# Two unused 32-byte tiles in the SBUF of an attention and gated-MLP kernel

## The chip, the cores and the metric

The kernel runs on one core of one Trainium2 chip. A core has a matrix engine (PE, with its weight loads shown as PEld), a vector engine (DVE), a scalar engine (ACT), a GpSimd engine (POOL) and a queue engine (SP) that only issues transfers. The on-chip memory that the engines compute from is the SBUF, 128 partitions wide; matmuls write to the PSUM. The metric is the device time of one execution in microseconds. Three runs of the kernel before gave 789.4, 789.5 and 789.96 us; the median is 789.5 us.

## The reference

Shapes: 8 batches, 8 heads, 576 rows of 64 elements, 32 memory slots. The attention output of one batch is 576 x 512, and all of them make 4608 rows of the gated MLP with 1536 inner columns.

```python
a = softmax(phi, over the rows)                # [b, h, 576, 32]
k_m = einsum('bhsm,bhsd->bhmd', a, k)
v_m = einsum('bhsm,bhsd->bhmd', a, v)
attn = softmax(q @ k_m.T / 8, over the slots)
x = (attn @ v_m) with the heads side by side   # [4608, 512]
gate = 1 / (1 + exp(-(x @ w_gate)))
out = (gate * (x @ w_val)) @ w_out             # [4608, 512]
```

All inputs and outputs are float32; the weights `w_gate`, `w_val`, `w_out` reach the kernel as 64-bit words, which it turns into float32 on the chip (`to_f32`).

## The kernel before

**The work.** The inner dimension 1536 is cut into 12 blocks of 128 (`f` = 0 to 11, constant `NFT`), and a batch's 576 rows into two halves: 256 rows (`c` = 0) and 320 rows (`c` = 1, of which the last 64 are a leftover). For each batch the attention weights `at` (softmaxed scores, transposed) are made once. Instead of forming x, the kernel multiplies `v_m` into the weight block: `make_u` (line 426) streams `wg`, the converted gate and value weights, past weights from `vT`, and gives U. `gate_half` (line 463) then streams `at` past U: 12 matmuls of 256 or 320 columns. Its sigmoid and product give `g`. `out_half` (line 499) streams a block of `w_out` past `g`: 6 matmuls of 512 columns, which accumulate in the banks `acc`. `out_left` (line 545) does the same for the leftover rows of two batches at a time.

**Two words for a number.** U, `at`, `g` and `w_out` are each kept as a high and a low part (`hi`, `lo`); a product is hi x hi, hi x lo and lo x hi, so each logical product takes three matmuls. These tiles have the type fp32r.

**The order.** 96 steps (batch, block) are written out by hand at line 753: batches 0 to 3 go in turns of four blocks with partial sums kept in DRAM (`part`), batches 4 to 7 go through all 12 blocks at once. A step is a gate half, an output half that belongs to a half three places earlier (`LAG` = 3), a second gate half and another output half; on every second step `make_u` stands between. The order on the matmul queue is fixed by `in_turn` (line 127), that of transfers by `move` (line 113). `convert` jobs for the weights end at step 30; the side work of the next batches' attention is put between the halves by `sides` (line 725). `again` (line 418) loads the `at` tiles of a batch back a turn before they are used.

**The placing.** Three pools hold the SBUF tiles, opened in the order `keep`, `att`, `moe` (lines 66 to 69); a pool `conv0`, later `late` and `conv1`, comes behind. A pool's tiles lie one behind the other in the order in which they are first asked for, each rounded up to a multiple of 32 bytes in a partition. By the sizes, this is where the start of each tile lies, in bytes past a multiple of 64 and of 128:

| pool: tiles | start, bytes | past 64 | past 128 |
|---|---|---|---|
| keep: `ident`, `tails`, `wg` | 16512, 17024, 18048 | 0 | 0 |
| keep: `wo_hi`, `wo_lo` (blocks 0 to 7) | 67200, 83584 | 0 | 0 |
| keep: `kT`, `vT` (5 buffers), `at_hi`, `at_lo` (2 each) | 99968 to 124544 | 0 | 0 |
| att: `z`, then `ph`, `kvt`, `kvm`, `q` | 124544, then 124576 on | 0, then 32 | 0, then 32 |
| att: `e` | 156864 | 0 | 64 |
| moe: `u_hi`, `u_lo`, `sg`, `g_lo`, `g_hi`, `left`, `wo_raw`, `row` | 161824 on | 32 | 32 |
| late: `wo2_hi`, `wo2_lo` (blocks 8 to 11) | 208672, 216864 | 32 | 32 |

All slices that the matmuls of the main loop take start a multiple of 256 bytes behind the start of their tile. The two w_out tiles differ only in the block they serve:

```python
wos = {0: [keep.tile([P, NE, DM], F32R, name=f"wo_{part}") for part in ("hi", "lo")]}   # NE = 8
def wo_of(f):
    return [t[:, f % NE, :] for t in wos[f // NE]]
```

The second is made at line 207, when the last conversion buffers are free. Names in the profile leave out numbers, so `wo_hi` there stands for `wo_hi` and `wo2_hi`.

Of the kernel before, what the change touches and what calls it, by code (L numbers as in the profile page):

```python
# [9 lines left out]
F32 = mybir.dt.float32  # L10
# [7 lines left out]
P = 128  # L18
# [34 lines left out]
def attn_moe_kernel(  # L53
# [12 lines left out]
    keep = ctx.enter_context(tc.tile_pool(name="keep", bufs=1))  # L66
    dram = ctx.enter_context(tc.tile_pool(name="dram", bufs=1, space=bass.MemoryType.DRAM))
    sb = ctx.enter_context(tc.tile_pool(name="att", bufs=1))
# [18 lines left out]
    ident = keep.tile([P, P], F32, name="ident")  # L87
    make_identity(nc, ident)

    tails = keep.tile([P, NG, P], F32, name="tails")  # L90
    nc.vector.memset(tails, 0.0)


    wg = keep.tile([P, NFT, NKT, 256], F32, name="wg")
    wos = {0: [keep.tile([P, NE, DM], F32R, name=f"wo_{part}") for part in ("hi", "lo")]}

    def wo_of(f):
# [746 lines left out]
```

## Time and profile before

| | |
|---|---|
| median of three runs | 789.5 us |
| profiled execution, first to last instruction (span) | 788.0 us |
| PE busy | 750.2 us, 95% |
| PEld busy | 617.4 us, 78% |
| DVE busy | 436.4 us, 55% |
| ACT busy | 335.8 us, 43% |
| moved by DMA | 93.17 MB, 118 GB/s on average |
| mean granted clock of the matrix engine | 0.981 |

The page gives the profiled execution's span alone, not its time from outside; the span lies 1.5 us under the median of the runs. Busy time counts an instruction from its start to its end, and matmuls overlap, so that the time of one in the trace is longer than the distance to the next. The pace of matmuls is therefore read from the starts, or from the rows of the chain of waits, in which a stretch of matmuls of one kind is merged into one row with its length and count.

### The profile page before, as it was taken

The numbers are of one execution on the slowest core, as the hardware profiler recorded it, in microseconds if no ns is written. First come the engines' busy times: TensorE is split into PE (matmuls) and PEld (weight loads), VectorE is DVE, ScalarE is ACT, GpSimd is POOL, SyncE is SP. The second block draws the span as 40 slices with busy tenths as digits, with TensorE's granted clock in tenths as the row PEclk, the third lists the DMA queues.
The fourth block names the chain that finished last, engine by engine and source line by source line (L and its number), as shares of the span: only waits on it lengthen the run. The fifth ranks groups of instructions, "written<-read, shape, count | busy, mean of one in ns | idle before, by whom it ended". The sixth has DMA issues, their size and how long they took to land.

```text
span 788.0 us, 13851 instructions
## 1 busy us (share of the span) xinstructions
PE 750.2 (95%) x5658; PEld 617.4 (78%) x5658; DVE 436.4 (55%) x840; ACT 335.8 (43%) x789; POOL 15.8 (2%) x34
## 2 busy tenths in 40 slices
PE   6866999989999999999999999999999999999997
PEld 4654777678788888887888878878888888888886
DVE  2878656887677775455654653365234553343432
ACT  3445455545644434332633543346333443333322
POOL 0000000000100000000000000000000000000000
PEclk9897899999999999999999999999999999999999
DMA  9683555564755555333253133002000100010001
GB/s 343 240 294 129 188 191 201 205 226 167 240 213 195 188 177 182 122 108 114 67 198 148 54 104 121 1 29 86 1 1 2 54 14 1 1 55 1 1 1 67
DMA packets 31231, 93.17 MB, mean 118 GB/s; under 512 B 3520, under 2 KB 4544, under 8 KB 29120
## 3 DMA queue, kind: packets, MB, share of 16 engines
q1 hardware_dynamic: 22528, 69.22, 24.3%
q0 software_dynamic: 4032, 14.68, 5.6%
q10 hardware_dynamic: 4608, 8.39, 3.5%
q8 instruction: 44, 0.72, 0.4%
q14 instruction: 19, 0.16, 0.1%
HBM read 69.73 MB, written 22.54 MB: 117 GB/s over the span
## 4 chain that ended last, share of the span: by engine, by line
PE 77%; DVE 9%; ACT 6%; DMA 5%; issue 2%; SPq 0%; ACTq 0%; DVEq 0%; POOLq 0%
PE pu_t L133 47%; PE acc L133 30%; DMA words<-in_wgv_dram 3%; ACT L108 2%; ACT ph L108 1%; DVE u_lo L123 1%; DVE q L394 1%; DVE e L373 1%; DVE sg L489 1%; DVE e L358 1%; DVE at_lo L123 1%; DMA part<-row 1%; ACT sg L108 1%; ACT e L108 1%; DMA ph<-in_phiT_dram 1%
## 5 line engine op out<-in xcount | busy, mean ns | idle before, releaser
L133 PE MATMUL pu_t<-at_hi,u_hi 128*128 128x256 f32 (+1 forms) x760 | 230.5, 303 | 7.6 <-ACT u_hi L437 5.1
L133 PE MATMUL pu_t<-at_hi,u_lo 128*128 128x256 f32 (+1 forms) x760 | 227.1, 299 | 3.8 <-DVE u_lo L123 3.8
L133 PE MATMUL pu_t<-at_lo,u_hi 128*128 128x256 f32 (+1 forms) x760 | 227.1, 299 | 1.6 <-DVE at_lo L123 1.6
L489 DVE TENSOR_TENSOR sg<-pu_t,sg 128x256 f32<-128x256 f32 (+1 forms) x190 | 86.5, 455 | 203.9 <-ACT sg L108 127.5
L108 ACT ACTIVATE sg<-pu_t 128x256 f32<-128x256 f32 (+1 forms) x190 | 78.0, 411 | 227.6 <-PE pu_t L133 214.5
L133 PEld LDWEIGHTS pu_t<-at_hi,u_hi 128*128 128x128 f32 x760 | 144.7, 190 | 20.8 <-ACT u_hi L437 6.0
L133 PE MATMUL acc<-wo_hi,g_hi 128*128 128x512 f32 x384 | 156.9, 409 | 0.1
L133 PE MATMUL acc<-wo_hi,g_lo 128*128 128x512 f32 x384 | 152.7, 398 | 0.0
L133 PEld LDWEIGHTS pu_t<-at_lo,u_hi 128*128 128x128 f32 x760 | 145.1, 191 | 8.9 <-DVE at_lo L123 1.8
L133 PE MATMUL acc<-wo_lo,g_hi 128*128 128x512 f32 x384 | 151.9, 396 | 0.0
L133 PEld LDWEIGHTS pu_t<-at_hi,u_lo 128*128 128x128 f32 x760 | 145.3, 191 | 4.8 <-DVE u_lo L123 4.8
L490 ACT CAST g_hi<-sg 128x256 fp32r<-128x256 f32 x192 | 77.9, 406 | 125.8 <-DVE sg L489 119.6
L123 DVE TENSOR_TENSOR g_lo<-sg,g_hi 128x256 fp32r<-128x256 f32 x192 | 80.8, 421 | 60.4 <-ACT g_hi L490 60.4
L133 PEld LDWEIGHTS acc<-wo_hi,g_hi 128*128 128x128 f32 x384 | 72.9, 190 | 49.0 <-issue 39.4
L133 PEld LDWEIGHTS acc<-wo_hi,g_lo 128*128 128x128 f32 x384 | 72.4, 189 | 16.7
L133 PEld LDWEIGHTS acc<-wo_lo,g_hi 128*128 128x128 f32 x384 | 73.0, 190 | 9.1
L123 DVE TENSOR_TENSOR u_lo<-pu_t,u_hi 128x512 fp32r<-128x512 f32 (+1 forms) x100 | 63.2, 662 | 3.9 <-ACT u_hi L437 2.5
L133 PE MATMUL pu_t<-wg,vT 64*32 64x512 f32 (+1 forms) x800 | 58.5, 596 | 5.1 <-DVE wg L199 5.1
L437 ACT CAST u_hi<-pu_t 128x512 fp32r<-128x512 f32 (+1 forms) x100 | 51.8, 571 | 1.7 <-PE acc L133 1.0
L515 DVE TENSOR_TENSOR row<-acc,row 128x512 f32<-128x512 f32 x32 | 21.9, 686 | 7.0 <-DMA row<-part 4.3
L108 ACT ACT_TABLE_LOAD x18 | 23.1, 1283 | 1.8 <-PEq L834 0.7
L133 PE MATMUL pu_t<-kvm,e 128*32 128x128 f32 x512 | 18.4, 288 | 5.2 <-ACT e L278 5.2
(93 smaller groups left out, 573.3 us busy)
## 6 DMA issues: line engine op xcount, KB each, us to landing
kvm<-in_kvm_dram SPq DMA_DIRECT2D x16, 1024.0 KB, 7.7
q<-in_qT_dram SPq DMA_DIRECT2D x16, 512.0 KB, 5.4
part<-row SPq DMA_DIRECT2D x32, 256.0 KB, 2.4
row<-part ACTq DMA_DIRECT2D x32, 256.0 KB, 3.0
out_dram<-row SPq DMA_DIRECT2D x32, 256.0 KB, 2.0
words<-in_wgv_dram POOLq DMA_DIRECT2D x12, 512.0 KB, 5.2
words<-in_wo_dram POOLq DMA_DIRECT2D x10, 512.0 KB, 5.3
ph<-in_phiT_dram SPq DMA_DIRECT2D x8, 576.0 KB, 4.1
```

The source lines that it names most:

```text
L108: last_act[0] = nc.scalar.activation(*args, **kw)
L123: return nc.vector.tensor_tensor(lo, x, hi.bitcast(F32), op=ALU.subtract)
L133: last_pe[0] = do(*args, **kw)
L358: nc.vector.tensor_tensor(e, e, mx.unsqueeze(3).broadcast_to([P, 2, w, M]), op=ALU.subtract)
L373: nc.vector.tensor_tensor(e, e, zs.unsqueeze(3).broadcast_to([P, 2, w, M]), op=ALU.mult)
L394: nc.vector.transpose(t.rearrange("p r n -> p (r n)"), loaded[b, "e"])
L437: nc.scalar.copy(hi[:, r, :nf], pb[r])
L489: last_prod[0] = nc.vector.tensor_tensor(prod[:, :n], ps[1][:, :n], sg[:, :n], op=ALU.mult)
L490: nc.scalar.copy(ghi, prod[:, : 2 * P])
L515: nc.vector.tensor_tensor(st, o, st, op=ALU.add)
```

## The change

Two tiles of 128 partitions x 8 float32 (32 bytes in a partition) are asked for and never used. `gap0` stands in the pool `keep` between `wg` and w_out's first tile; `gap1` is the first tile of the pool `att`, ahead of `z`. Everything in `keep` from `wo_hi` on (w_out's first tile, `kT`, `vT`, `at_hi`, `at_lo`) starts 32 bytes later, and everything in `att`, `moe` and behind starts 64 bytes later. No instruction is added, removed or put elsewhere.

```diff
     make_identity(nc, ident)
 
+    sb.tile([P, 8], F32, name="gap1")
     tails = keep.tile([P, NG, P], F32, name="tails")
     nc.vector.memset(tails, 0.0)
 
 
     wg = keep.tile([P, NFT, NKT, 256], F32, name="wg")
+    keep.tile([P, 8], F32, name="gap0")
     wos = {0: [keep.tile([P, NE, DM], F32R, name=f"wo_{part}") for part in ("hi", "lo")]}
```

## The prediction, as it was put on record

> **What bounds the kernel now.** I read the profile page first, its busy times, its row of the granted clock and its shares of the chain that ended last:
>
> ```profile
> span 788.0 us, 13851 instructions
> PE 750.2 (95%) x5658; PEld 617.4 (78%) x5658; DVE 436.4 (55%) x840; ACT 335.8 (43%) x789; POOL 15.8 (2%) x34
> ...
> PEclk9897899999999999999999999999999999999999
> ...
> PE pu_t L133 47%; PE acc L133 30%; DMA words<-in_wgv_dram 3%; ACT L108 2%; ACT ph L108 1%; DVE u_lo L123 1%; DVE q L394 1%; DVE e L373 1%; DVE sg L489 1%; DVE e L358 1%; DVE at_lo L123 1%; DMA part<-row 1%; ACT sg L108 1%; ACT e L108 1%; DMA ph<-in_phiT_dram 1%
> ```
>
> The matmul queue is busy 95% of the span, and 77% of the last chain is matmuls into `pu_t` and `acc`. From the sixth of the forty slices on the clock is in its top tenth, so it is no term here. What matters is how far apart two matmuls of the main loop start. The groups of the matmul queue by shape say how many there are (count, then total busy time and mean of one; these durations overlap, so the mean is not the pace):
>
> ```profile
> L133 PE MATMUL acc<-wo_hi,g_hi 128*128 128x512 f32 x384 | 156.9, 409 | 0.1
> ...
> L133 PE MATMUL pu_t<-at_hi,u_hi 128*128 128x320 f32 x380 | 120.1, 316 | 1.2 <-DVE sg L489 1.0
> ...
> L133 PE MATMUL pu_t<-at_hi,u_hi 128*128 128x256 f32 x380 | 110.4, 290 | 6.5 <-ACT u_hi L437 5.1 <-ACT at_hi L404 1.4
> ...
> L133 PE MATMUL pu_t<-wg,vT 64*32 64x512 f32 x736 | 53.5, 611 | 0.2 <-DVE wg L199 0.2
> ...
> L133 PE MATMUL pu_t<-wo_hi,u_hi 128*128 128x512 f32 x48 | 18.9, 393 | 0.0
> ```
>
> In a name the streamed tile stands before the loaded weights: `acc<-wo_hi,g_hi` streams 512 columns of w_out past weights of `g_hi`. Each such row has two sisters (hi/lo), so there are 3 x 384 = 1152 output matmuls of 512 columns, 2304 gate matmuls (192 halves of 12) of 256 or 320 columns that stream `at`, and 3 x 48 = 144 matmuls of 512 columns for the leftover rows. All go back to back: the idle column is near zero. The pace comes from the chain of waits in order of time (start, length, instructions merged), here from batches 6 and 7:
>
> ```profile
> 652.16 1.40 PE acc L133 x6
> 653.56 1.43 PE pu_t L133 x12
> ...
> 656.40 1.76 PE pu_t L133 x12
> 658.16 1.40 PE acc L133 x6
> ...
> 665.37 1.40 PE acc L133 x6
> ...
> 678.57 1.38 PE acc L133 x6
> ...
> 682.79 1.76 PE pu_t L133 x12
> 684.55 1.38 PE acc L133 x6
> 685.92 2.46 PE pu_t L133 x28
> 688.38 1.59 PE acc L133 x6
> ...
> 691.74 1.38 PE acc L133 x6
> ...
> 704.91 1.40 PE acc L133 x6
> ```
>
> Up to 678.57 the output halves use the first w_out tile (blocks 0 to 7), from 678.57 to 704.91 the second (`wo2`, blocks 8 to 11), and at 704.91 batch 7 is back at the first. Two steps of the loop take 665.37 - 652.16 = 13.21 us and 678.57 - 665.37 = 13.20 us with the first tile, but 691.74 - 678.57 = 13.17 us and 704.91 - 691.74 = 13.17 us with the second. The instructions are the same; by the tile sizes the first tile starts at a multiple of 128 bytes, the second 32 bytes past one, and the weights (`g`, `u`) 32 bytes past one in both. The change shifts the first tile by just 32. So the trace of before already holds a trial of one part of the change.
>
> The leftover matmuls show the same without gate matmuls between. The timeline of the matmul queue (start, length):
>
> ```profile
> 751.76 0.39 PE L133 MATMUL pu_t<-wo_hi,u_hi 128*128 128x512 f32 x1
> ...
> 757.36 0.28 PE L133 MATMUL pu_t<-at_hi,u_hi 128*128 128x256 f32 x1
> ```
>
> ```profile
> 383.26 0.39 PE L133 MATMUL pu_t<-wo_hi,u_hi 128*128 128x512 f32 x1
> ...
> 385.98 0.28 PE L133 MATMUL pu_t<-at_hi,u_hi 128*128 128x256 f32 x1
> ```
>
> ```profile
> 450.20 0.40 PE L133 MATMUL pu_t<-wo_hi,u_hi 128*128 128x512 f32 x1
> ...
> 452.96 0.28 PE L133 MATMUL pu_t<-at_hi,u_hi 128*128 128x256 f32 x1
> ```
>
> First: 24 matmuls on the first tile in 5.60 us, 233.3 ns each. Second and third: 12 on the second tile in 2.72 and 2.76 us, 226.7 and 230.0 ns each.
>
> **The change part by part.** It adds and removes no instruction and no wait; it changes start addresses.
>
> *w_out's first tile, 0 to 32 bytes past a multiple of 64.* 8 batches x 8 blocks = 64 of the 96 steps use it, that is 32 pairs of steps. At the pace of the second tile each pair of steps gains 0.03 to 0.04 us; I take 0.04: 32 x 0.04 = 1.3 us. The leftover rows use it in 4 x 24 = 96 matmuls; against the mean of the two second-tile runs, 228.3 ns, they gain 5.0 ns each: 0.5 us. Term: -1.8 us. Bounds: 0 (the gap is not due to the 32 bytes), and -5.7 us if every one of the 768 + 96 matmuls fell from 233.3 to 226.7 ns. One gap stays: the weights move by 64 at the same time, so this tile and its weights will lie 32 and 96 bytes past a multiple of 128, where the trial had 32 and 32.
>
> *`at_hi` and `at_lo`, the gate's streamed tiles, also 0 to 32.* No run of before streams `at` from there. Three paces are known: 256 columns 1.43/12 = 119.2 ns, 320 columns 1.76/12 = 146.7 ns, 512 columns at best 226.7 ns. They lie on one line: 27.5 ns for 64 columns is 0.43 ns a column, 80.0 ns for the next 192 is 0.42. So the gate matmuls already run at the pace that w_out reaches only when shifted, and I take 0 for them. Bounds: a loss of 6.6 ns each, the distance between w_out at 0 and at 32 turned round, is 2304 x 6.6 ns = 15.2 us. A gain is bounded by the cheapest excess in sight: a block of 12 gates and 6 outputs on the second tile still takes 1.38 us for the six, 230 ns each, 3.3 ns above the line; with streams alike on both sides of the switch that might go, 384 x 3.3 ns = 1.3 us, beside the 5.7 us above.
>
> *`vT` 0 to 32, `wg` stays.* The 50 groups of u matmuls (one starts at 647.71, the next output matmul at 648.73) cost 1.02 us each:
>
> ```profile
> 647.71 1.09 PE L133 MATMUL pu_t<-wg,vT 64*32 64x512 f32 x16
> 648.73 0.50 PE L133 MATMUL acc<-wo_hi,g_hi 128*128 128x512 f32 x1
> ```
>
> Their stream does not move and their weights do. If what counts is how stream and weights lie to each other, they get the slower case: 6.6/226.7 = 2.9% of 51 us is 1.5 us lost; the gain is bounded by the same 1.5 us. I take 0, since only the weights shift and each is a narrow strip (64 rows by 32 columns). `kT` against `q` goes from unlike to like and has fewer matmuls: within that bound.
>
> *Everything later, by 64.* Its offset from a multiple of 64 stays: 0. *ACT, DVE and the queues:* casts into the first and the second w_out tile stand in one row, 617 to 629 ns, so their cost does not see the 32 bytes:
>
> ```profile
> L216 ACT CAST wo_hi<-wo_raw x12: 617/620/629, 49.0 to 298.5; 128x512 fp32r<-128x512 f32 x12
> ```
>
> Transfers of 576 KB into `at` (at 0) and into `ph` (at 32) land in 3.8, 4.9 and 4.1 us, with no order by offset:
>
> ```profile
> ph<-in_phiT_dram SPq DMA_DIRECT2D x8, 576.0 KB, 4.1
> at_hi<-at SPq DMA_DIRECT2D x8, 576.0 KB, 3.8
> at_lo<-at SPq DMA_DIRECT2D x8, 576.0 KB, 4.9
> ```
>
> They are issued a whole turn of four steps (some 26 us) before their use, so even 1 us more stays covered; without that cover 8 turns would pay 8 us.
>
> Sum: -1.8 + 0 + 0 + 0 = -1.8 us on the profiled 788.0 us span. That execution lies 1.5 us under the median of 789.5 us (what comes before and after the first and last instruction); taken from the median, **787.7 us**.
>
> **The rivals.**
>
> *Both streams lie alike (faster by more).* The second-tile pairs still pay above the line after each gate block. If that comes from switching between a stream at 0 and one at 32, it ends: 1152 + 144 output matmuls at 226.7 ns. Gain 5.7 us on the first tile and 1.3 us on the second: 782.5 us. For it: 226.7 ns is reached only in the run at 383.26. Against it: the run at 450.20 has no gates between and still has 230.0.
>
> *The gate pays (slower).* The shift takes `at` off its multiple of 64. If a stream at 32 carries in the gate what w_out's shifted tile still carries in the loop, 3.3 ns above the line, the 2304 matmuls lose 7.6 us: 789.5 - 1.8 + 7.6 = 795.3 us. It decides from 0.8 ns a gate matmul on, where 2304 x 0.8 ns eats the 1.8 us. For it: the shifted w_out is itself not free of excess in the loop, and no idle time stands before the gate that could take it up. Against it: the line, on which 226.7 ns was reached at an offset of 32.
>
> *The 32 bytes are not the cause.* The second tile also lies elsewhere (some 208 KB into the partition, the first at 67 KB); if the place makes the 0.04 us, and not the offset, nothing moves: 789.5 us. For it: the trace has no tile at the same place with another offset. Against it: nothing but the sharpness of the step at 678.57. [...]
>
> *The tiles are never placed.* Nothing uses them, and if they take no room, all stays: 789.5 us. Against it is only that a tile is asked for.
>
> **How the numbers follow.** A measurement here can tell about 0.2%, 1.6 us, from no change. Forecast: 0.36, with its own range 786.3 to 789.0 us (of it 0.24 faster, 0.10 same, 0.02 slower). Both alike: 0.20, faster. Gate pays: 0.23, of which 0.22 slower, 0.01 same. Not the cause: 0.16, and never placed: 0.05 (0.18 same, 0.02 slower, 0.01 faster by small effects of the places). That gives faster 0.45, same 0.29, slower 0.26. The range goes from 783.0 us, just inside the first rival, to 794.5 us, just under the gate's rival; past the ends lie the far halves of these two.
>
> **What would show it.** Right: pairs of steps take 13.17 us in blocks 0 to 7 too, the 24 leftover matmuls about 228 ns each, and the gate rows stay 1.43 and 1.76 us. The first rival: output blocks of 1.36 us everywhere. The gate's: rows of twelve above 1.45 or 1.78 us. No cause: 1.40 and 13.20 us as before. Wrong altogether: a stall that is new, since none is added here.

## The result, and the profile after

The changed kernel takes 785.8 us (785.07 to 786.25 us in four runs) against 789.69 us for the kernel before: a ratio of 0.9948 with a 95% interval of 0.9928 to 0.9968, so 3.9 us less. Timed once more among the experiments, beside further runs of the kernel before, it was at 0.9962 (0.9943 to 0.9981). The profiled execution took 786.25 us with a span of 784.5 us. The page of the changed kernel, its busy times:

```profile
span 784.5 us, 13851 instructions
PE 745.7 (95%) x5658; PEld 613.1 (78%) x5658; DVE 436.6 (56%) x840; ACT 336.2 (43%) x789; POOL 15.8 (2%) x34
```

The same 13851 instructions; the matmul queue is busy 4.5 us less, DVE and ACT are as before. Where it went shows in the chain of waits of the changed kernel, in the stretch that the prediction read (start, length, instructions merged; the helper's line is now 135):

```profile
650.81 1.41 PE pu_t L135 x12
652.22 1.39 PE acc L135 x6
653.61 1.76 PE pu_t L135 x12
655.37 1.39 PE acc L135 x6
...
668.48 1.39 PE acc L135 x6
...
675.65 1.40 PE acc L135 x6
...
681.61 1.39 PE acc L135 x6
683.00 2.43 PE pu_t L135 x28
...
694.72 1.39 PE acc L135 x6
```

Two steps with w_out's first tile take 668.48 - 655.37 = 13.11 us, where they took 13.20 to 13.21 us. Output blocks went from 1.40 to 1.39 us, as forecast. The gate blocks of 256 columns went from 1.43 to 1.41 us, which was not forecast; those of 320 columns stay at 1.76 us. On w_out's second tile, from 675.65 on, two steps take 694.72 - 681.61 = 13.11 us instead of 13.17 us: its output blocks are slower (1.39 instead of 1.38 us), and the gate more than makes up for it. The 24 leftover matmuls of the last pair, in the timeline of the matmul queue:

```profile
748.39 0.39 PE L135 MATMUL pu_t<-wo_hi,u_hi 128*128 128x512 f32 x1
...
753.88 0.28 PE L135 MATMUL pu_t<-at_hi,u_hi 128*128 128x256 f32 x1
```

5.49 us, 228.8 ns each instead of 233.3 ns.

By these rows, 32 pairs of steps gain 0.10 us each, the 16 pairs on w_out's second tile 0.06 us each, and 96 leftover matmuls 4.5 ns each. That is an estimate of 3.2 + 1.0 + 0.4 = 4.6 us, inside the 2.5 to 5.7 us that the interval of the ratio allows.

The two spans can't be compared to less than a few us. One wait of the chain, for an output row's transfer, is 2.48 us in the kernel before and 4.31 us in the changed one:

```profile
376.83 2.48 DMA out_dram<-row
```

```profile
373.48 4.31 DMA out_dram<-row
```

The first hundred us, in which the two chains wait 24.3 us (10.09 + 4.22 + 10.03, before) and 18.7 us (9.78 + 8.89, changed) for `words<-in_wgv_dram`, vary too: in two profiles of the changed kernel the first output matmul starts at 61.68 and at 59.93 us, in that of the kernel before at 59.79 us. So the readings below go by the rows of the loop and, for the sum, by the ratios.

### The profile page after: what moved, and what is told of

Read it like the earlier page. It is cut to its first block, busy times and chain, and to the rows that moved or that the text cites. A ratio compares the mean times of both kernels' runs of the same rounds, so it can differ in the third digit from the quotient of the medians.

```text
span 784.5 us, 13851 instructions
## 1 busy us (share of the span) xinstructions
PE 745.7 (95%) x5658; PEld 613.1 (78%) x5658; DVE 436.6 (56%) x840; ACT 336.2 (43%) x789; POOL 15.8 (2%) x34
## 4 chain that ended last, share of the span: by engine, by line
PE 77%; DVE 9%; ACT 6%; DMA 4%; issue 2%; SPq 0%; ACTq 0%; DVEq 0%; POOLq 0%
PE pu_t L135 47%; PE acc L135 30%; DMA words<-in_wgv_dram 2%; ACT L110 2%; ACT ph L110 1%; DVE u_lo L125 1%; DVE q L396 1%; DVE e L375 1%; DVE sg L491 1%; DVE e L360 1%; ACT sg L110 1%; DVE at_lo L125 1%; DMA part<-row 1%; DMA out_dram<-row 1%; ACT e L110 1%
## 5 line engine op out<-in xcount | busy, mean ns | idle before, releaser
L135 PEld LDWEIGHTS pu_t<-wg,vT 64*32 64x32 f32 x800 | 10.3, 105 | 17.1 <-DVE wg L201 7.0
```

Source lines behind the costliest of these rows:

```text
L135: last_pe[0] = do(*args, **kw)
```

## The experiments

Each moves tiles by unused tiles of 32 to 128 bytes and changes nothing else. For reading them it helps to have, for each stream, the **distance** from the start of the streamed tile to the start of its weights, past a multiple of 256 bytes; all slices in the loop and all buffers keep it. In the kernel before it is 160 for `at` to `u` and for w_out's first tile to `g` and `u`, and 0 for w_out's second tile. In the changed kernel it is 192, 192 and 0.

**w_out's first tile alone.**

```diff
     wg = keep.tile([P, NFT, NKT, 256], F32, name="wg")
+    keep.tile([P, 8], F32, name="gap0")
     wos = {0: [keep.tile([P, NE, DM], F32R, name=f"wo_{part}") for part in ("hi", "lo")]}
+    keep.tile([P, 8], F32, name="gap2")
```

> Only w_out's first tile goes to 32 bytes past a multiple of 64; at, kT and vT move by 64 and so stay at 0, everything later moves by 64 as in the changed kernel. Theory A (what counts is how far past a multiple of 64 bytes a streamed tile starts): output blocks of six go from 1.40 to about 1.38 us in blocks 0 to 7, gate rows of twelve stay at 1.43 and 1.76 us, two loop steps take 13.17 us in all blocks, time about 787.9 us (the 1.8 us of the prediction). Theory B (what counts is whether stream and weights start alike past 64): the same here. Theory C (the place of the tile counts, not the 32 bytes): 1.40 us and 789.7 us as before.

Measured: 788.62 us, ratio 0.9979 (0.9959 to 1.0), 1.7 us less, with an interval that just reaches no change; the rows say more. Its chain, blocks 0 to 7:

```profile
654.41 1.43 PE pu_t L135 x12
655.85 1.39 PE acc L135 x6
```

Output blocks as in the changed kernel, gate blocks as before: the forecast term by itself, near its forecast size. The place of the tile on a large scale is not the cause.

**`at` alone.**

```diff
+    sb.tile([P, 8], F32, name="gap1")
     tails = keep.tile([P, NG, P], F32, name="tails")
...
     def new_at(b):
+        if not at:
+            keep.tile([P, 8], F32, name="gap0")
```

> Only at_hi and at_lo go to 32 past a multiple of 64; w_out's first tile, kT and vT stay where they were, everything later moves by 64. Theories A and B: gate rows of 256 columns go from 1.43 to 1.41 us, 320 columns stay at 1.76, output blocks stay at 1.40 us; 96 x 0.02 = 2 us gained, about 787.7 us. If the gain of the changed kernel needs both streams alike: gate rows stay at 1.43 us and the time at 789.7 us. Theory C: no change.

Measured: 788.2 us, ratio 0.9975 (0.9956 to 0.9994), 2.0 us less. Its chain:

```profile
652.19 1.41 PE pu_t L134 x12
653.61 1.39 PE acc L134 x6
```

The gate's gain is there with w_out's first tile unmoved, and by their middle values the two parts add up to the whole (0.21% and 0.25% of 0.52%; each is known to about 0.2%). But the output blocks are at 1.39 us here as well, though w_out's first tile did not move and, by theory A, should have kept 1.40 us. What did move under it is `g`, by 64. So the 2.0 us are not the gate's alone.

**Only what lies behind moves, by 32.**

```diff
+    sb.tile([P, 8], F32, name="gap1")
     tails = keep.tile([P, NG, P], F32, name="tails")
```

> The streamed tiles at and w_out's first tile stay at 0; everything from the second pool on moves by 32, so that the weights u and g, and w_out's second tile, now start at a multiple of 64 too. Theory B (stream and weights alike): as good as the changed kernel, 785.8 us, gate rows 1.41 us, output blocks 1.39 us. Theory A (the stream's own offset): gate rows 1.43 us, output blocks 1.40 us in all twelve blocks, so slower than before by 16 x 0.04 = 0.6 us: 790.3 us.

Measured: 786.46 us, ratio 0.9953 (0.9933 to 0.9974). Its chain:

```profile
649.77 1.41 PE pu_t L134 x12
651.19 1.39 PE acc L134 x6
...
654.34 1.39 PE acc L134 x6
...
667.45 1.39 PE acc L134 x6
```

Every row of the changed kernel, two steps in 13.11 us, with streams that start at a multiple of 64 as before. The streams' own offset is not what counts; theory A falls. Distances: 192, 192, 0, as in the changed kernel.

**Only the tile ahead of w_out.**

```diff
     wg = keep.tile([P, NFT, NKT, 256], F32, name="wg")
+    keep.tile([P, 8], F32, name="gap0")
```

> Only the tile ahead of w_out: w_out's first tile, kT, vT and at go from 0 to 32, as in the changed kernel, but the weights u and g go from 32 to 64 past a multiple of 128 instead of to 96. Theory A (the stream's own offset past 64): as the changed kernel, gate rows 1.41 us, output blocks of the first tile 1.39 us, 785.8 us. Theory B (stream and weights alike past 64) and theory B2 (the one bad distance from stream to weights is 32 past a multiple of 128): the distance is 32 as before, so gate rows 1.43 to 1.44 us, output blocks 1.40 us, time as before.

Measured: 790.05 us, ratio 1.0001 (0.9983 to 1.002). Its chain:

```profile
655.18 1.40 PE acc L134 x6
656.58 1.44 PE pu_t L134 x12
...
668.38 1.40 PE acc L134 x6
```

The streams have moved just as in the changed kernel, and nothing is gained: 13.20 us for two steps, as before. Streams and weights moved together, the distances are the old ones. So of the change's two tiles the one in the second pool does the work, and the one ahead of w_out does nothing that these runs can tell: with it alone the time is as before, and without it as after.

**w_out's second tile alone, to a multiple of 64.**

```diff
             late = ctx.enter_context(tc.tile_pool(name="late", bufs=1))
+            late.tile([P, 8], F32, name="gap2")
```

> The kernel before with w_out's second tile alone (and the last conversion buffer) moved by 32, to a multiple of 64. Theories A and B: its output blocks go from 1.38 to 1.40 us, two steps take 13.21 us in all blocks, 16 x 0.04 us and 48 leftover matmuls x 5 ns lost: about 0.9 us, 790.6 us. Theory C (its place makes it faster): 1.38 us as before and 789.7 us.

Measured: 791.05 us, ratio 0.9999 (0.9982 to 1.0016): the total can't tell. The chain, from 681.40 on with the second tile:

```profile
681.40 1.39 PE acc L133 x6
...
687.38 1.40 PE acc L133 x6
```

Its blocks after a gate of 320 columns go from 1.38 to 1.39 or 1.40 us, and two steps take 13.19 us, where they took 13.17 us before and 13.21 us on the first tile. The tile has stayed in its region and lost half of its lead, so place alone was not it; its distance is now 224.

**Only `g` moves.**

```diff
+        if last_prod[0] is None:
+            mb.tile([P, 8], F32, name="gap2")
         sg = mb.tile([P, S - 2 * P], F32, name="sg", bufs=3)
```

> No streamed tile of the gate or of w_out's first tile moves, and u does not: only g (and what lies behind it, w_out's second tile too) moves by 32. If the distance from stream to weights counts: output blocks of the first tile 1.385 us (distance 192, as in the changed kernel), gate rows 1.43 to 1.44 us as before, leftover matmuls on the first tile, whose weights are u, 233 to 236 ns as before, and on the second tile, where the distance becomes 224, 233 instead of 227 to 230 ns; time about 788.3 us. If the place of the streamed tile counts: output blocks 1.40 us.

Measured: 788.35 us, ratio 0.9978 (0.9959 to 0.9997). Its chain:

```profile
652.06 1.39 PE acc L133 x6
653.45 1.43 PE pu_t L133 x12
654.88 1.38 PE acc L133 x6
```

and the timeline of its matmul queue, around 12 leftover matmuls on the second tile:

```profile
382.14 0.40 PE L133 MATMUL pu_t<-wo_hi,u_hi 128*128 128x512 f32 x1
...
384.94 0.28 PE L133 MATMUL pu_t<-at_hi,u_hi 128*128 128x256 f32 x1
```

w_out's first tile lies exactly where it lay, and its output blocks run at 1.39 and 1.38 us because their weights moved. The leftovers on the second tile, whose weights `u` did not move with it, take 2.80/12 = 233.3 ns, where the same stretch took 226.7 ns before. The output blocks on the first tile are the plainest case of all the runs: same stream, same instruction, other weights' address, other pace. Of what moved along with `g`, the matmuls read only w_out's second tile. With nothing but their weights moved, the six matmuls took 1.39 and 1.38 us instead of 1.40 and 1.41 us (in the kernel before, the row at 652.16 and the one after the next gate):

```profile
654.99 1.41 PE acc L133 x6
```

**Other distances.** Streams stay, everything from the second pool on moves by 64, 96 or 128.

```diff
+    sb.tile([P, 16], F32, name="gap1")      # then 24, then 32 elements
     tails = keep.tile([P, NG, P], F32, name="tails")
```

> The streams at and w_out's first tile stay at 0; the weights u and g go from 32 to 96 past a multiple of 128 (everything from the second pool on moves by 64). Theory B (alike past 64): 0 against 32 past 64 as before, so gate rows 1.43 us, output blocks 1.40 us, time as before. Theory B2 (only the distance 32 past a multiple of 128 is slow): distance 96, gate rows 1.41 us, output blocks 1.39 us, about 785.8 us. In the run with at alone moved, w_out's first tile stood at this distance and took 1.39 us.

> The streams at and w_out's first tile stay at 0; the weights u and g go from 32 to a multiple of 128 (everything from the second pool on moves by 96). Distance 0 for all three streams. Theories B and B2: fast, gate rows 1.41 us, output blocks 1.38 to 1.39 us, 785.8 us or a little less, since w_out's second tile took 1.38 us at this distance in the kernel before.

> The streams at and w_out's first tile stay at 0; everything from the second pool on moves by 128, so the weights stay 32 past a multiple of 128, and move against the streams by 128. If only what is left past 128 counts (B, B2): as before, gate rows 1.43 us, output blocks 1.40 us, time as before. If the distance counts past 256 or more: another pace, up to the 4 us of the changed kernel.

Measured: 788.75, 788.52 and 788.05 us, ratios 0.9984 (0.9967 to 1.0001), 0.9977 (0.9958 to 0.9996) and 0.9976 (0.9958 to 0.9994). The chains, in this order:

```profile
650.75 1.40 PE acc L134 x6
652.15 1.40 PE pu_t L134 x12
...
663.88 1.40 PE acc L134 x6
```

```profile
652.59 1.39 PE acc L134 x6
653.98 1.43 PE pu_t L134 x12
...
656.80 1.75 PE pu_t L134 x12
...
665.73 1.39 PE acc L134 x6
```

```profile
651.71 1.39 PE acc L134 x6
653.10 1.43 PE pu_t L134 x12
...
664.87 1.39 PE acc L134 x6
```

The totals can't rank these three; the rows can. The last 24 leftover matmuls of each, on w_out's first tile, in the timelines of the matmul queue (in the same order):

```profile
749.85 0.40 PE L134 MATMUL pu_t<-wo_hi,u_hi 128*128 128x512 f32 x1
...
755.45 0.28 PE L134 MATMUL pu_t<-at_hi,u_hi 128*128 128x256 f32 x1
```

```profile
751.76 0.39 PE L134 MATMUL pu_t<-wo_hi,u_hi 128*128 128x512 f32 x1
...
757.20 0.28 PE L134 MATMUL pu_t<-at_hi,u_hi 128*128 128x256 f32 x1
```

```profile
750.92 0.40 PE L134 MATMUL pu_t<-wo_hi,u_hi 128*128 128x512 f32 x1
...
756.52 0.28 PE L134 MATMUL pu_t<-at_hi,u_hi 128*128 128x256 f32 x1
```

They take 5.60, 5.44 and 5.60 us. Two steps on the first tile, and these 24, against the distance of `at` and w_out (all of the runs in which both are alike on that tile):

| distance | kernel | two steps | gate, 256 columns | output block | leftover matmul |
|---|---|---|---|---|---|
| 160 | before; only the tile ahead of w_out; second tile alone | 13.20 to 13.21 us | 1.43 to 1.44 us | 1.40 to 1.41 us | 233.3 ns |
| 192 | changed, twice; behind by 32 | 13.11 to 13.12 us | 1.41 us | 1.39 us | 228.8 to 229.2 ns |
| 224 | behind by 64 | 13.13 us | 1.40 us | 1.40 us | 233.3 ns |
| 0 | behind by 96 | 13.14 us | 1.43 us | 1.39 us | 226.7 ns |
| 32 | behind by 128 | 13.16 us | 1.43 us | 1.39 us | 233.3 ns |

These leftover matmuls, which run with no gate between them, go as B says: the distances that are a multiple of 64 (192 and 0) are fast, the other three are slow alike. (On the second tile, at distance 0, stretches of twelve spread from 226.7 to 230.8 ns each.) In the loop, where gate and output take turns, neither theory holds as it was put. "Alike past 64" (B) would have distance 224 as slow as 160 and 0 as fast as 192; "only 32 past 128 is slow" (B2) would have distance 32 as slow as 160. The kernel before stood at the worst of the five distances, the changed one stands at the best, and the others lie between. The gate and the output blocks do not rank the distances alike.

**A mixed placing.**

```diff
+    sb.tile([P, 16], F32, name="gap1")
     tails = keep.tile([P, NG, P], F32, name="tails")
...
     wos = {0: [keep.tile([P, NE, DM], F32R, name=f"wo_{part}") for part in ("hi", "lo")]}
+    keep.tile([P, 8], F32, name="gap0")
```

> Distances, from the start of a streamed tile to the start of its weights, past a multiple of 256: before 160 for at and for w_out's first tile, 0 for its second. Here the tiles from kT on move by 32 and everything from the second pool on by 96, so that at to u is 224 (where the run with everything behind moved by 64 had gate rows of 1.40 us), w_out's first tile to g is 0 and its second 0 (where leftover matmuls took 227 ns). If each stretch's pace goes by its own distance: gate rows 1.40 and 1.76 us, output blocks 1.385 us, two steps 13.10 us, leftovers 227 ns, time about 785.3 us, a little less than the changed kernel. If neighbouring stretches set each other's pace: output blocks up to 1.40 us and no better than the changed kernel.

> The changed kernel once more, beside the mixed one on the same chip: gate rows 1.41 us, output blocks 1.39 us, 0.5% less time than before.

Measured: 785.07 us, ratio 0.9948 (0.9927 to 0.9968), and for the changed kernel beside it 786.99 us, 0.9962 (0.9943 to 0.9981). The intervals overlap: the mixed kernel is not shown to be faster. Its chain and the timeline of 24 leftover matmuls:

```profile
653.29 1.40 PE acc L135 x6
...
660.47 1.40 PE acc L135 x6
661.87 1.41 PE pu_t L135 x12
663.28 1.38 PE acc L135 x6
...
666.42 1.40 PE acc L135 x6
```

```profile
427.11 0.39 PE L135 MATMUL pu_t<-wo_hi,u_hi 128*128 128x512 f32 x1
...
432.32 0.39 PE L135 MATMUL pu_t<-wo_hi,u_lo 128*128 128x512 f32 x1
```

From the first to the last of the 24 are 5.21 us over 23, 226.5 ns: as expected of distance 0. But in the loop the output block after the 320-column gate takes 1.40 us, not 1.385, and two steps take 666.42 - 653.29 = 13.13 us, not 13.10. In these runs a stretch's pace goes with its neighbour's distance too. The output blocks of the run with `at` alone moved had hinted it: at distance 224 they took 1.39 us beside gates at 192, where those of the run by 64 took 1.40 us beside gates at 224. w_out's second tile shows the same. Its own distance is 0 in the kernel before, in the changed one and in the runs with everything behind moved by 64, 96 and 128, yet its block after a 320-column gate takes 1.38, 1.39, 1.40, 1.39 and 1.36 us. The last of these, from the chain of the run by 128:

```profile
684.00 1.36 PE acc L134 x6
...
697.09 1.36 PE acc L134 x6
```

Two steps take 13.09 us there, the shortest in any of the runs, with the gate at distance 32.

## Why the prediction was right, and where it was not

The forecast of 787.7 us had the direction and the place; the range holds 785.8 us. The gain was 3.9 us instead of 1.8, and 785.8 us lies below the forecast's own range of 786.3 to 789.0 us: the whole range held it because it reached down to the first rival.

- **What bounds the kernel**: held. DVE and ACT did as much work as before (436.6 us against 436.4, 336.2 against 335.8), and the time followed the pace of the matmuls: 3.9 us less, with 4.5 us less of busy matmul queue.
- **w_out's first tile, -1.8 us**: held in size. Moved alone, it gave 1.7 us (0 to 3.2 us by the interval); in the changed kernel the leftovers gained 233.3 - 228.8 = 4.5 ns each where 5.0 was put.
- **`at`, taken as 0**: this step failed. By the rows of the changed kernel it is 96 blocks x 0.02 us = 1.9 us; the run with `at` moved alone gained 2.0 us, a part of it in the output blocks. The reason given was that 256, 320 and 512 columns lay on one line and the gate therefore ran at the best pace already. The line was no floor: 256 columns went from 119.2 to 1.41/12 = 117.5 ns, and to 1.40/12 = 116.7 ns at distance 224. Three points that happen to be in line were taken for a limit.
- **Why the shift works**: failed as put, and came right by luck of the arithmetic. The sum rested on the stream's own offset; the run with the tile ahead of w_out alone has that offset and gains nothing (790.05 us). What the rows of these runs go by is the distance between stream and weights, that of the neighbouring stretch included: with the streams unmoved and the distance at 192 the time was 786.46 us. The prediction named that gap (32 and 96 past 128, where its trial had 32 and 32) and gave it no weight.
- **Everything later by 64, taken as 0**: so this term was no bystander. The 64 bytes against 32 are what changes the distance; without the tile in the second pool the gain is gone (ratio 1.0001).
- **`vT`, taken as 0**: held. The u matmuls took 1.02 us; the stretch of gate and u matmuls at 683.00 now takes 2.43 us, of which 1.41 us are gate, which leaves 1.02 us.
- **ACT and the queues at no cost**: held; ACT is busy 336.2 us against 335.8, and the transfers into `at` land in 3.8 and 4.8 us against 3.8 and 4.9.
- **The rivals**: "both streams lie alike" had the right sense that the gate and the output belong together, but its 1.36 us blocks did not come in the changed kernel; they stand only in the run by 128, after 320-column gates on the second tile. "The gate pays" has the opposite sign. "The 32 bytes are not the cause" and "never placed" are out by the runs with one tile moved.

What stays open: why the pace depends on the distance, and by what period. The runs show five distances 32 bytes apart and no more. The run in which only `g` moved shows that the weights' address alone shifts the pace, by 0.01 to 0.03 us in a block of six; by what mechanism, no row of these traces shows. A rule by multiples of 64 fits the leftover matmuls and not the loop, where distance 32 takes 13.16 us for two steps and 160 takes 13.20 us; how neighbouring stretches act on each other is not shown. Nor do the runs settle why the first hundred us differ between profiles.

## What to carry to other kernels

Where matmuls run back to back and the matmul queue is the bound, measure the distance between starts by tile and not only by shape: the same instruction at two addresses differed here by 3% (226.7 against 233.3 ns), and a trace that streams two tiles past like weights already holds the trial. Then move the weights against the streams and not the streams by themselves; a few steps of 32 bytes in an unused tile are a cheap sweep. Sweep the loop itself: here a stretch of matmuls of one kind ranks the distances otherwise than the loop in which two kinds take turns. A pace that fits one line with other shapes is not thereby at its limit.

## What the runs showed that was not expected

In these runs the pace of a matmul went with where the weights of its neighbourhood lie relative to its stream: 226.7 to 233.3 ns for 512 columns, 116.7 to 120.0 ns for 256 (rows of 1.40 to 1.44 us), while twelve of 320 columns take 1.75 us at distance 0 and 1.76 us at 160 and 192. Without gates between, the last 24 leftover matmuls on w_out's first tile take 226.7 to 229.2 ns each at distances 0 and 192, and 233.3 ns at 32, 160 and 224. Moving streams and weights together leaves the rows of the loop as they were.
